# Linear attention and a multiplicative FFN on one core: a new slot plan for key features, query transposes and two numerators

## The chip, the cores and the metric

The kernel runs on one core of a Trainium2 chip. The metric is the device time in microseconds: the median of the runs of a kernel. The kernel before takes 248.61 us (three runs, 248.41 to 248.72).

## The reference

Eight batches of eight heads, 576 positions, head size 64. Queries and keys go through a ReLU and are multiplied by a cosine and by a sine of the position, which gives 128 features:

```python
    q_p = phi(q, cos_w, sin_w)
    k_p = phi(k, cos_w, sin_w)
    kv = np.einsum('bhsf,bhsd->bhfd', k_p, v)
    z = np.sum(k_p, axis=2)
    num = np.einsum('bhsf,bhfd->bhsd', q_p, kv)
    den = np.einsum('bhsf,bhf->bhs', q_p, z)[..., None] + 1e-06
```

The attention output `num / den` is laid out as 4608 tokens of 512 features and goes through an FFN without a nonlinearity: `h = (x @ w1) * (x @ w2)`, then `h @ w3 @ w_out`, where `w1` and `w2` are 512 x 1024, `w3` is 1024 x 1024 and `w_out` is 1024 x 512.

## The kernel before

Tokens pass the FFN in nine tiles of 512. `w3 @ w_out` is computed once, so a tile is: `x @ w1` and `x @ w2` (L465), a copy of the first product out of PSUM by ScalarE (L518), their product by VectorE into `abT` (L522), the output matmuls (L535), and a copy of the output by ScalarE (L542). The matmuls run in bf16.

Attention for a batch is cut into five chunks of positions (four of 128 rows, one of 64; odd batches take the chunk of 64 first). The steps for a chunk, and their names:

- key features, `prep_k`: cosine half on VectorE (L273), sine half on ScalarE (L277). They need the load of `ks`, which comes in two halves of the partitions; the chunk of 64 rows needs the first half alone.
- values copied by GpSimd, `prep_v` (L300).
- `kv_chunk` (L308): matmuls that sum keys times values over all five chunks in PSUM; the sum is copied to `kvs` (L313, L314).
- query features and their transpose, `prep_q`: features as for keys, then a transposing DMA from SyncE's queue into `qpT` (L286).
- numerators, `num` (L368): eight matmuls with `qpT` and `kvs`, then a normalization on VectorE in three instructions (L384 to L386) into `xblk`, which is read by `x_tr`, a transposing DMA (L416) on the same SyncE queue. This makes the `xT` that the FFN tiles read.

The order of the work is written out by hand. `ffn_groups` is a generator: after each group of matmuls of a tile (about four matmuls of 512 columns) it yields, and at that point the calls that are listed for this slot run, so attention instructions are put into each engine's queue between FFN instructions. There are 232 slots: 40 for tile 0, then 24 for each tile, 16 of L465 and 8 of L535. So slots 40 to 63 are tile 1, 64 to 87 tile 2, 88 to 111 tile 3, and so on. `plan` (L572) puts the five chunks of a batch at the slots given: `kf` for key features, `vc` for value copies, `kv` for the key-value sums, `qf` for query features with their transposes, `nu` for numerators. `plan_loads` (L584) places the loads of `k`, `q` and `v`, in halves. A load is held back by a tiny copy on ScalarE that GpSimd, whose queue issues the loads, waits for (L568, L570).

Batches 4 to 7 share one pattern: `last` is the slot of the first numerators of the batch before, `base` that of its own, and the places are offsets to one or the other. Every engine works its queue in the order that results, so an instruction that waits holds back all that stands behind it.

Of the kernel before, what the change touches and what calls it, by code (L numbers as in the profile page):

```python
# [68 lines left out]
def kernel(  # L69
# [176 lines left out]
    def order_of(b):  # L246

        return [0, 1, 2, 3, 4] if b % 2 == 0 else [4, 0, 1, 2, 3]
# [40 lines left out]
    def prep_k(b, c):  # L289
        features(b, feat_of(b)[0], raw[b, "k"], c)  # L290

    def prep_q(b, c):
        features(b, feat_of(b)[1], raw[b, "q"], c)
        if c in dma_q(b):
            transpose_q(b, c)

    def prep_v(b, c):
        R = ROWS[c]
        eng = nc.vector if b < 2 else nc.gpsimd
        eng.tensor_copy(out=feat_of(b)[2][:R, c, :, 0:D], in_=raw[b, "v"][:R, :, c, :])  # L300

    def kv_chunk(b, c, i):
        kp, qp, va = feat[b]
        if i == 0:
            att_of(b)["kv"] = ps_att.tile([P, 2, 512], FP32, name="pnum")
        kvt = att[b]["kv"]
        for h in range(H):
            nc.tensor.matmul(kvt[:, h // 4, ds((h % 4) * 65, 65)], lhsT=kp[:, c, h, :],  # L308
                             rhs=va[:, c, h, 0:D + 1], start=(i == 0 and h % 4 == 0),
                             stop=(i == NCH - 1 and h % 4 == 3))  # L310
        if i == NCH - 1:
            kvs = sm.tile([P, H, D + 1], BF16, name="kvs", bufs=2)
            nc.scalar.copy(out=kvs[:, 0:4, :], in_=kvt[:, 0, 0:260])  # L313
            nc.vector.tensor_copy(out=kvs[:, 4:8, :], in_=kvt[:, 1, 0:260])  # L314
            att[b]["kvs"] = kvs
# [88 lines left out]
    def x_tr(b, c, by_vector=False):  # L404
        R, rows = ROWS[c], out_rows(b, c)
        xblk = att[b]["x"].pop(c)
        xf = xblk[:].rearrange("p g h d -> p (g h d)")
        if b % 2 == 0:
            slot = S * b + 128 * c
        else:  # L410
            slot = S * b + (0 if c == 4 else 64 + 128 * c)
        t, o = divmod(slot, 512)
        if t not in xT:
            xT[t] = xtp.tile([P, 4, 512], BF16, name="xT")
        if b >= 2 or (b, c) in ((0, 4), (1, 3)):
            nc.sync.dma_start_transpose(out=xT[t][:, :, ds(o, R)], in_=xf[rows])  # L416
            return
        pst = ps_tr.tile([P, 8, 128], BF16, name="pst")
        for kc in range(4):
            nc.tensor.transpose(pst[:, kc, :], xf[:, ts(kc, 128)], identb[:])  # L420
        copy = nc.vector.tensor_copy if by_vector else nc.scalar.copy
        copy(out=xT[t][:, :, ds(o, R)], in_=pst[:, 0:4, rows])
# [139 lines left out]
    def at(s, *calls):  # L562
        slots[s] += calls
# [8 lines left out]
    def plan(b, kf, vc, kv, qf, nu, loads=None, xt=None):  # L572
        order = order_of(b)
        for i, c in enumerate(order):
            at(kf[i], lambda c=c: prep_k(b, c))
            at(qf[i], lambda c=c: prep_q(b, c))
            at(vc[i], lambda c=c: prep_v(b, c))
        for i, c in enumerate(order):
            at(kv[i], lambda c=c, i=i: kv_chunk(b, c, i))
        for i, c in enumerate(order):  # L580
            at(nu[i], lambda c=c: num(b, c, in_two=b == 1 and c in (0, 2)))
            at(xt[i] if xt else nu[i], lambda c=c: x_tr(b, c, by_vector=(b, c) == (1, 1)))

    def plan_loads(b, when):  # L584

        for piece, s in zip([(n, half) for n in {2: "kv", 3: "qkv"}.get(b, "kqv") for half in range(2)], when):
            def issue(piece=piece):
                hold_back()
                load(b, *piece)
            at(s, issue)  # L590
# [42 lines left out]
    for jp, s in enumerate((12, 16, 18, 20, 22, 24, 26, 28)):  # L633
# [3 lines left out]
         qf=(29, 30, 30, 31, 31), nu=(35, 36, 38, 39, 42), xt=(37, 38, 40, 42, 42))  # L637
    for c, s in zip(order_of(1), (31, 32, 34)):
# [3 lines left out]
    plan(2, kf=(37, 39, 40, 41, 44), vc=(41, 42, 43, 44, 45), kv=(46, 46, 46, 47, 47),  # L642
         qf=(41, 42, 43, 45, 46), nu=(48, 50, 52, 57, 60))
    plan_loads(3, (36, 37, 47, 50, 54, 57))
    plan(3, kf=(54, 57, 59, 61, 63), vc=(64, 65, 66, 67, 68), kv=(71, 71, 72, 72, 72),
         qf=(60, 62, 64, 67, 70), nu=(74, 77, 79, 84, 87))

    bases = [74, 99, 123, 148, 173]
    for b, last, base in zip(range(4, B), bases, bases[1:]):
        plan_loads(b, [last + s for s in (-11, -7, -4, 3, 6, 9)])  # L650
        plan(b, kf=[last + s for s in (3, 6, 8, 11, 13)],
             vc=[base + s for s in (-9, -8, -7, -6, -5)],
             kv=[base + s for s in (-4, -3, -3, -2, -2)],
             qf=[base + s for s in (-11, -9, -6, -4, -1)],
             nu=[base + s for s in (0, 2, 5, 8, 11)])

    for i in range(2 * (NT - 1)):
# [42 lines left out]
```

## Time and profile before

| what | value |
|---|---|
| time, median of three runs | 248.61 us |
| the profiled execution | 247.98 us, span 246.2 us |
| TensorE, share of the span | 97% |
| VectorE | 57% |
| ScalarE | 53% |
| GpSimd | 38% |
| HBM traffic over the span | 196 GB/s |

The share of the span is busy time; the ends of matmuls in the profile are modelled and overlap the next ones, so for TensorE it is read together with the starts of its instructions. The granted TensorE clock is full throughout. The chain of work that ended last is followed back from the end of the kernel; a line in it that is not TensorE's is a place where TensorE waited.

### The profile page before, as it was taken

The numbers are of one execution on the slowest core, as the hardware profiler recorded it, in microseconds if no ns is written. First come the engines' busy times: TensorE is split into PE (matmuls) and PEld (weight loads), VectorE is DVE, ScalarE is ACT, GpSimd is POOL, SyncE is SP. The second block draws the span as 40 slices with busy tenths as digits, with TensorE's granted clock in tenths as the row PEclk, the third lists the DMA queues.
The fourth block names the chain that finished last, engine by engine and source line by source line (L and its number), as shares of the span: only waits on it lengthen the run. The fifth ranks groups of instructions, "written<-read, shape, count | busy, mean of one in ns | idle before, by whom it ended". The sixth has DMA issues, their size and how long they took to land.

```text
span 246.2 us, 5011 instructions
## 1 busy us (share of the span) xinstructions
PE 238.2 (97%) x1842; PEld 130.7 (53%) x1872; DVE 139.3 (57%) x344; ACT 130.6 (53%) x266; POOL 94.2 (38%) x196
## 2 busy tenths in 40 slices
PE   8799999999999999999999999999999999999994
PEld 3479555566964445545554545455545544444443
DVE  7775663668975645655665575678466645312420
ACT  2675324856944873566367555754575333434332
POOL 7655352124412171218022804261303005978800
PEclk9999999999999999999999999999999999999999
DMA  7999999999989989999999999999996437988923
GB/s 192 179 197 199 207 206 201 192 185 167 167 146 143 164 117 164 155 124 136 177 161 133 142 140 162 158 132 169 151 120 122 63 64 219 256 284 282 284 109 128
DMA packets 86200, 41.22 MB, mean 167 GB/s; under 512 B 53792, under 2 KB 82720, under 8 KB 86176
## 3 DMA queue, kind: packets, MB, share of 16 engines
q0 software_dynamic: 37008, 27.20, 72.4%
q1 hardware_dynamic: 49168, 13.71, 38.0%
q8 instruction: 14, 0.23, 0.4%
q14 instruction: 10, 0.08, 0.1%
HBM read 38.80 MB, written 9.44 MB: 196 GB/s over the span
## 4 chain that ended last, share of the span: by engine, by line
PE 89%; DMA 5%; ACT 2%; DVE 1%; issue 1%; ACTq 0%
PE ffnps L465 48%; PE ffnps L535 24%; PE ffnps L240 6%; PE pnum L368 4%; PE pnum L308 4%; DMA ks<-in_k_dram 3%; DMA kf<-in_k_dram 3%; PE pst L226 1%; ACT kp L277 1%; PE pst L339 1%; PE pst L420 1%; PE ffnps L551 1%; PE kva L325 0%; DVE xblk L386 0%; DVE abT L522 0%
## 5 line engine op out<-in xcount | busy, mean ns | idle before, releaser
L465 PE MATMUL ffnps<-xT,w2b 128*128 128x512 bf16 (+2 forms) x337 | 75.0, 343 | 0.5
L465 PE MATMUL ffnps<-xT,w1b 128*128 128x512 bf16 (+2 forms) x335 | 74.5, 343 | 0.3
L522 DVE TENSOR_TENSOR abT<-asb,ffnps 128x512 bf16<-128x512 bf16 x64 | 43.9, 685 | 47.1 <-PE ffnps L465 44.8
L535 PE MATMUL ffnps<-w34b,abT 128*128 128x512 bf16 x270 | 63.6, 379 | 0.8 <-DVE abT L522 0.3
L518 ACT CAST asb<-ffnps 128x512 bf16<-128x512 f32 x64 | 37.4, 585 | 50.0 <-PE ffnps L465 42.8
L570 POOL COPY seen<-mark 1x1 bf16<-1x1 bf16 x50 | 9.2, 183 | 99.6 <-ACT mark L568 99.6
L465 PEld LDWEIGHTS <-w2b 128*128 128x128 bf16 x344 | 31.0, 98 | 27.3
L465 PEld LDWEIGHTS <-w1b 128*128 128x128 bf16 x344 | 30.9, 98 | 26.4
L535 PEld LDWEIGHTS <-abT 128*128 128x128 bf16 x280 | 25.9, 98 | 28.3 <-DVE abT L522 0.8
L542 ACT COPY osb<-ffnps 128x512 f32<-128x512 f32 x35 | 20.5, 585 | 34.8 <-PE ffnps L535 34.8
L277 ACT ACTIVATE qp<-qs,sinv 128x512 bf16<-128x512 bf16 (+2 forms) x40 | 28.1, 716 | 1.3 <-DMA qs<-in_q_dram 1.3
L386 DVE TENSOR_TENSOR xblk<-pnum,den 128x512 bf16<-128x512 f32 (+1 forms) x37 | 25.6, 691 | 1.3
L277 ACT ACTIVATE kp<-ks,sinv 128x512 bf16<-128x512 bf16 (+1 forms) x35 | 25.0, 720 | 1.6 <-DMA ks<-in_k_dram 1.6
L450 POOL DMA_DIRECT2D out_dram<-osb x42 | 22.1, 531 | 3.3 <-issue 2.5
L300 POOL COPY va<-vs 128x512 bf16<-128x512 bf16 (+1 forms) x30 | 17.4, 619 | 7.9 <-DMA vs<-in_v_dram 7.9
L368 PEld LDWEIGHTS <-qpT 128*128 128x128 bf16 x320 | 15.4, 98 | 8.6 <-DVE qpT L353 0.6
L384 DVE TENSOR_SCALAR den<-pnum 128x8 f32<-128x8 f32 (+1 forms) x37 | 6.1, 164 | 23.7 <-PE pnum L368 23.5
L273 DVE TENSOR_SCALAR qp<-qs,cosv 128x512 bf16<-128x512 bf16 (+1 forms) x40 | 18.6, 472 | 0.6 <-DMA qs<-in_q_dram 0.5
L368 PE MATMUL pnum<-kvs,qpT 128*128 128x65 bf16 x296 | 15.7, 194 | 0.1
L240 PE MATMUL ffnps<-woutb,w3T 128*128 128x512 bf16 x61 | 15.1, 379 | 0.2
L308 PEld LDWEIGHTS <-kp 128*128 128x128 bf16 x280 | 11.3, 98 | 3.8
L273 DVE TENSOR_SCALAR kp<-ks,cosv 128x512 bf16<-128x512 bf16 (+1 forms) x35 | 12.1, 358 | 1.7 <-DMA ks<-in_k_dram 1.6
(88 smaller groups left out, 182.6 us busy)
## 6 DMA issues: line engine op xcount, KB each, us to landing
out_dram<-osb POOLq DMA_DIRECT2D x16, 256.0 KB, 4.5
out_dram<-osb POOLq DMA_DIRECT2D x24, 128.0 KB, 4.0
qs<-in_q_dram POOLq DMA_DIRECT2D x8, 256.0 KB, 7.3
ks<-in_k_dram POOLq DMA_DIRECT2D x6, 320.0 KB, 7.0
qs<-in_q_dram POOLq DMA_DIRECT2D x6, 320.0 KB, 8.4
vs<-in_v_dram POOLq DMA_DIRECT2D x6, 320.0 KB, 6.0
ks<-in_k_dram POOLq DMA_DIRECT2D x6, 256.0 KB, 7.8
vs<-in_v_dram POOLq DMA_DIRECT2D x6, 256.0 KB, 5.9
```

Of the source, the lines that this page charges most:

```text
L240: nc.tensor.matmul(acc[:, :], lhsT=w3T[:, lc % 4, :], rhs=woutb[:, lc, :], start=(lc == 0), stop=(lc == 7))
L273: nc.vector.tensor_scalar(out=dst[:R, c, :, 0:D], in0=src[:R, :, c, :], scalar1=0.0, scalar2=cosv[:R, at:at + 1], op0=ALU.max, op1=ALU.mult)
L277: nc.scalar.activation(out=dst[:R, c, 0:n, D:F], in_=src[:R, 0:n, c, :], func=ACTF.Relu, scale=sinv[:R, at:at + 1], bias=0.0)
L308: nc.tensor.matmul(kvt[:, h // 4, ds((h % 4) * 65, 65)], lhsT=kp[:, c, h, :], rhs=va[:, c, h, 0:D + 1], start=(i == 0 and h % 4 == 0), sto ...
L368: nc.tensor.matmul(banks[h // 4][:, ds((h % 4) * 65, 65)], lhsT=qpT[:, h, ds(at, 128)], rhs=kvs[:, h, :], start=True, stop=True)
L386: nc.vector.tensor_tensor(out=xblk[rows, g], in0=n4[:, :, :, 0:D], in1=den[rows, g].unsqueeze(3).to_broadcast([R, G, 4, D]), op=ALU.mult)
L450: eng.dma_start(out=rows[:, :, cols], in_=osb[64 * i:64 * i + rows.shape[0], :, cols])
L465: nc.tensor.matmul(out, lhsT=w[:, kc, ts(jc, 128)], rhs=x[:, kc, tok], start=(kc == 0), stop=(kc == 3))
L518: nc.scalar.copy(out=asb[:], in_=aT[:, :])
L522: nc.vector.tensor_mul(out=abT[:, jc, :], in0=asb[:], in1=bT[:, :])
L535: nc.tensor.matmul(ops[:, :], lhsT=abT[:, jc, ts(ms, 128)], rhs=w34b[:, jc, :], start=(jc == 0), stop=(jc == 7))
L542: nc.scalar.copy(out=osb[:, ms % 2, :], in_=ops[:, :])
```

## The change

It gives other slots to attention work. In batch 3 the first key features move from slot 54 to 56, and the second and third numerators from 77 and 79 to 76 and 78. In batches 4 to 7 the key features after the first come one or two slots sooner, and the query features with their transposes one or two slots sooner, so that the last of them is at three slots ahead of the first numerators where it was one slot ahead. The aim is that data that pass through transposing transfers are there in time, and that a feature that waits for its load stands less in the way.

```diff
-    plan(3, kf=(54, 57, 59, 61, 63), vc=(64, 65, 66, 67, 68), kv=(71, 71, 72, 72, 72),
-         qf=(60, 62, 64, 67, 70), nu=(74, 77, 79, 84, 87))
+    plan(3, kf=(56, 57, 59, 61, 63), vc=(64, 65, 66, 67, 68), kv=(71, 71, 72, 72, 72),
+         qf=(60, 62, 64, 67, 70), nu=(74, 76, 78, 84, 87))
...
-        plan(b, kf=[last + s for s in (3, 6, 8, 11, 13)],
+        plan(b, kf=[last + s for s in (3, 5, 7, 9, 11)],
              vc=[base + s for s in (-9, -8, -7, -6, -5)],
              kv=[base + s for s in (-4, -3, -3, -2, -2)],
-             qf=[base + s for s in (-11, -9, -6, -4, -1)],
+             qf=[base + s for s in (-12, -10, -8, -6, -3)],
              nu=[base + s for s in (0, 2, 5, 8, 11)])
```

## The prediction

> **What bounds the kernel now.** I read the busy line of the page first, then the chain that ended last, then the list of waits, and last the timelines of TensorE and VectorE around the one wait in the middle. In order:
>
> ```profile
> PE 238.2 (97%) x1842; PEld 130.7 (53%) x1872; DVE 139.3 (57%) x344; ACT 130.6 (53%) x266; POOL 94.2 (38%) x196
> PE 89%; DMA 5%; ACT 2%; DVE 1%; issue 1%; ACTq 0%
> ```
>
> TensorE is busy 97% of the span and holds 89% of the chain that ended last. The modelled ends of matmuls overlap, so this busy share can hide small stalls; I measured them by starts. In steady stretches a 128x512 matmul starts 0.216 us after the one before it (four in 0.86 us). From 58 us to the last matmul at 243 us, every interval fits this rhythm (or twice it, at some twenty places where one record is missing) save two: 0.10 us at 70.3 us, ahead of batch 2's first numerator, and a larger one at 79 us. All else that a change in the middle of this kernel can win is that one, or lies in what this profile does not show. In the chain, the span of 246.2 us loses its time to transfers in two places:
>
> ```profile
> 0.74 6.18 DMA kf<-in_k_dram
> ...
> 70.72 7.33 DMA ks<-in_k_dram
> 78.11 0.28 issue
> 78.39 0.67 DVE abT L522
> 79.11 0.39 PE ffnps L535
> ```
>
> The first is the start-up, untouched here. The second is batch 3's key load, of which the chain says that it released VectorE, and VectorE released TensorE. The timelines, TensorE and then VectorE (start, duration, what; in brackets the idle time before it and who ended it):
>
> ```profile
> 76.24 1.03 PE L465 MATMUL ffnps<-xT,w2b 128*128 128x512 bf16 x4
> 77.11 1.67 PE L535 MATMUL ffnps<-w34b,abT 128*128 128x512 bf16 x7
> 79.11 0.39 PE L535 MATMUL ffnps<-w34b,abT 128*128 128x512 bf16 x1 [0.33 <-DVE abT L522]
> 79.33 0.42 PE L368 MATMUL pnum<-kvs,qpT 128*128 128x65 bf16 x8
> ```
>
> ```profile
> 75.76 0.68 DVE L522 TENSOR_TENSOR abT<-asb,ffnps 128x512 bf16<-128x512 bf16 x1
> 78.07 0.39 DVE L273 TENSOR_SCALAR kp<-ks,cosv 64x512 bf16<-64x512 bf16 x1 [1.63 <-DMA ks<-in_k_dram]
> 78.39 0.66 DVE L522 TENSOR_TENSOR abT<-asb,ffnps 128x512 bf16<-128x512 bf16 x1
> ```
>
> VectorE reached batch 3's first key feature (L273) at 76.44, and the load landed only at 78.05. Behind it stood the last product (L522) of FFN tile 1, though its inputs were there by about 77.3 (the w2 group starts at 76.24 and is over in about 1.03). The eighth output matmul needs that product. Seven matmuls from 77.11 put the eighth at 77.11 + 7 x 0.216 = 78.62; it started at 79.11. **The stall is 0.49 us** (0.33 as the profile counts it, since the modelled end of the seventh covers the rest). The waits list has nothing else of this kind, and for the query transposes that the change moves nothing but start-up work:
>
> ```profile
> DVE kp L273 <- DMA ks<-in_k_dram: 1.6, 1, 1.6
> PEld L535 <- DVE abT L522: 0.8, 1, 0.8
> PEld L368 <- DVE qpT L353: 0.6, 2, 0.4
> ```
>
> **What the Trainium skill says.** "TensorE: Matmul & The Clock Gate", section "Wait — 56ns, not 53.3ns?": start to start is N / 2.4 GHz + 2.5 ns, 215.7 ns at 512 columns. The trace agrees (0.216), so the matmul stream has no rate left to win. "Perfetto Trace Analysis", "Tensor Engine Instruction (MATMUL, LD_WEIGHTS)": matmul ends are estimated, and VectorE and ScalarE queues are strictly first in, first out. The trace agrees: the ready product waited behind the key feature. "DMA: Bandwidth & Descriptors", "Anatomy of one DMA — SWDGE (gpsimd) path": 2.0 us + bytes / 436e3, for 320 KB an estimate of 2.8 us. The trace disagrees: this load took 7.33, and the page's median for such loads is 7.0; I use the trace. Same page, "Issuing engines are not separate DMA queues": transposes and loads share 16 engines, which agrees with transposes taking 2.8 to 10.1 us between 131 and 176 us while loads run.
>
> **The change part by part.** No instruction is added or removed; the orders of GpSimd's and SyncE's queues stay as they were. Only places in the TensorE, VectorE and ScalarE orders move.
>
> Batch 3's first key chunk, slot 54 to 56. On VectorE the last product now stands ahead of the key feature. It can start at about 77.3 and end by 78.0, ahead of 78.62. TensorE gains 0.49 us. The wait is not gone: the feature still waits for 78.05, now with batch 2's fourth normalization (slot 57) behind it on VectorE. Its numerators run at 78.84 in the new clock (79.33 less 0.49), so VectorE is free first. On ScalarE the output copy of slot 57 stands behind the sine half, which ends at 78.8; its bank is reused only at slot 64, seven slots or some 6 us later. The second key chunk, slot 57 in both, waits for the second half (landed 80.87), now up to 0.49 us longer; behind it are output copies and batch 2's last normalization, none of which TensorE needs before slot 64. Cost nothing; **sum -0.49 us**.
>
> Batch 3's second and third numerators, slots 77 and 79 to 76 and 78. TensorE does the same eight matmuls each, 0.26 us, one 0.86 us group sooner. What is new: the third normalization (0.17 + 0.20 + 0.69, about 1.05 us) stands ahead of the last product of tile 2 on VectorE. On the old clock: numerators at 99.76, normalization free at 101.25, product 101.25 to 101.93; the output matmul that needs it issues at 100.89 + 7 x 0.216 = 102.40. Slack 0.4 us, so cost nothing (upper bound: if everything slips by 0.5, 0.1 us). What it buys: transposed x of batch 3's third chunk landed at 107.72, and tile 3 begins at 108.31, a slack of 0.6 us that grows by 0.8.
>
> Key features of batches 4 to 7, one or two slots sooner. Each is 0.36 on VectorE and 0.72 on ScalarE, beside output matmuls. Both halves of keys have landed before the first feature in each batch, by 3 us in batches 5 to 7; in batch 4 the second half lands at 98.62 and the first feature, whose slot does not change, runs on ScalarE at 98.65. That one is tight in both kernels. Cost nothing.
>
> Query features and transposes, one or two slots sooner. The second halves of q landed at 104.0, 129.0, 153.4 and 176.4; the first features ran at 109.8, 132.4, 157.0 and 181.0. One slot (about 0.9 us) fits. ScalarE then has a cast (0.58) and a feature (0.72) in each pair of slots of 1.73 us, VectorE 0.69 and 0.36; both fit. What it buys, by the completions in the trace: batch 5's fourth transpose landed at 150.29 for numerators at 150.90, batch 6's third and fourth at 171.66 and 174.75 for 172.19 and 175.04. Slacks of 0.6, 0.5 and 0.3 us grow by up to 1.7. In this profile that is worth zero. In the timed runs it may not be: their median, 248.61, is 0.63 above the profiled execution's 247.98, and late transfers are one thing that can fill this. Bounds 0 and 0.63; I take a fifth, 0.13, since fixed differences between the executions can fill it as well and three runs within 0.31 us do not look like chance stalls. This fifth is a judgment.
>
> Sum: -0.49 - 0.13 = -0.62, so 248.61 - 0.62 = **248.0 us**.
>
> **The rivals.**
> (A) The forecast, 248.0. For it: one stall, its cause named, its waiting product freed. Against: 0.49 is 0.197% of the time, at the very edge of what can be told, so all of the verdict hangs on the last tenths.
> (B) Only the stall, or part of it. The load's landing sets its size: if keys land 0.2 us earlier in timed runs, the stall there is 0.3. Then 248.61 - 0.3 to 0.49, about 248.2. For it: nothing else shows in the profile.
> (C) The near misses are real stalls in the timed runs. Then 0.49 + 0.63 = 1.12, 247.5. For it: three transposes within 0.6 us of their use; against: none stalls in the profile.
> (D) Slower. The transposes, packed two slots apart, take longer against the key loads issued at the same time, or the normalization ahead of tile 2's last product makes a new stall when batch 4's keys land late. A miss of about 1 us in one batch less the 0.49 gives +0.5, 249.1. For it: the tight landing at 98.62. Against: moves are all towards earlier, and the slacks above.
>
> **How the numbers follow.** A 0.50, B 0.27, C 0.13, D 0.10. Faster by over 0.2% (below 248.11): C and most of A, 0.42 + 0.13 = 0.55. Within: the rest of A, B, and 0.02 of D, 0.37. Slower: 0.08. The range leaves out half of C's and most of D's weight: 247.4 to 248.6.
>
> **What would show it.** The key-feature wait no longer stands ahead of the last product of tile 1, and the eighth output matmul follows at the 0.216 rhythm; the chain goes through no ks load in the middle; query transposes of batches 5 and 6 land 1 to 2 us ahead of their numerators; TensorE shows no new interval over 0.3 us. A new wait of an L535 or L368 matmul, or a span less than 0.3 us shorter, would prove me wrong.

## The result, and the profile after

The changed kernel takes 247.76 us (median of 15 runs, 247.51 to 248.43) against 248.72 us for the kernel before (15 runs, 247.67 to 249.65). The ratio is 0.9963, 95% interval 0.9949 to 0.9976: 0.9 us faster, and the spread of the runs is less than half as wide (0.9 us for 2.0). Two later comparisons of the same two kernels, below, gave a smaller gain, 0.6 to 0.7 us. Three later runs that took over 1.5% more than the fastest of their kernel, at a lowered clock, are left out of medians, means, counts and ratios: two of the kernel before and one of the larger dose.

The page of the changed kernel, its busy line and the line of the chain that ended last:

```profile
PE 238.0 (97%) x1842; PEld 130.7 (53%) x1872; DVE 138.2 (56%) x344; ACT 130.3 (53%) x266; POOL 94.1 (38%) x196
PE 92%; DMA 3%; issue 1%; DVE 1%; POOL 1%; ACT 0%; POOLq 0%
```

TensorE's share of the chain rises from 89% to 92%, and DMA's falls from 5% to 3%: a start-up load, now of queries and not of keys, is the only transfer left in it. The timelines of TensorE and VectorE around the old stall (start, duration, what; idle time before it in brackets):

```profile
76.39 1.03 PE L465 MATMUL ffnps<-xT,w2b 128*128 128x512 bf16 x4
77.25 1.89 PE L535 MATMUL ffnps<-w34b,abT 128*128 128x512 bf16 x8
78.98 0.42 PE L368 MATMUL pnum<-kvs,qpT 128*128 128x65 bf16 x8
```

```profile
75.91 0.68 DVE L522 TENSOR_TENSOR abT<-asb,ffnps 128x512 bf16<-128x512 bf16 x1
77.52 0.69 DVE L522 TENSOR_TENSOR abT<-asb,ffnps 128x512 bf16<-128x512 bf16 x1 [0.94 <-PE ffnps L465]
78.94 0.34 DVE L273 TENSOR_SCALAR kp<-ks,cosv 64x512 bf16<-64x512 bf16 x1 [0.72 <-DMA ks<-in_k_dram]
```

The eight output matmuls now stand in one row, x8 in 1.89 us, where they were x7 and, after a gap, x1. The product (L522) runs when TensorE has finished its inputs, at 77.52, and the key feature waits after it: 0.72 us on VectorE for 1.63 before. In total the two engines wait longer for key loads than before, where either waited 1.6 us, because in this execution the second half landed later too: VectorE waits 1.8 us and ScalarE 2.1 us for it.

```profile
ACT kp L277 <- DMA ks<-in_k_dram: 4.1, 3, 2.1
DVE kp L273 <- DMA ks<-in_k_dram: 2.5, 2, 1.8
```

The first half of batch 3's keys was issued at 70.86 and landed at 78.91, after 8.05 us for 7.33 in the profile of before. The second half landed at 82.29, after 8.42 us for 7.15. In the old order, by an estimate from the durations in the profile of before, the landing of the first half would have put the product at 79.27 to 79.93 and the eighth matmul at 79.98 for 78.76, a stall of 1.2 us. VectorE and ScalarE wait more for keys than they did, and TensorE does not wait for them at all: from 50 us on, its only interval out of rhythm is the 0.10 us at 70.4 that was there before.

The profiled spans differ by 0.34 us (246.22 and 245.88), not by 0.9: one execution each, and the changed one began its FFN 0.14 us later (first L465 at 16.01 for 15.87), so 0.34 + 0.14 is the 0.49 us stall to within 0.01.

### The profile page after: what moved, and what is told of

It is laid out like the page before. It is cut to its first block, busy times and chain, and to the rows that moved or that the text cites. A ratio compares the mean times of both kernels' runs of the same rounds, so it can differ in the third digit from the quotient of the medians.

```text
span 245.9 us, 5011 instructions
## 1 busy us (share of the span) xinstructions
PE 238.0 (97%) x1842; PEld 130.7 (53%) x1872; DVE 138.2 (56%) x344; ACT 130.3 (53%) x266; POOL 94.1 (38%) x196
## 4 chain that ended last, share of the span: by engine, by line
PE 92%; DMA 3%; issue 1%; DVE 1%; POOL 1%; ACT 0%; POOLq 0%
PE ffnps L465 50%; PE ffnps L535 24%; PE ffnps L240 6%; PE pnum L368 4%; PE pnum L308 4%; DMA qs<-in_q_dram 3%; PE pst L226 1%; PE pst L339 1%; PE pst L420 1%; PE ffnps L551 1%; POOL vs L133 0%; DVE xblk L386 0%; PE pfirst L368 0%; PE ffnps L368 0%; DVE qpT L353 0%
## 5 line engine op out<-in xcount | busy, mean ns | idle before, releaser
L465 PE MATMUL ffnps<-xT,w2b 128*128 128x512 bf16 (+2 forms) x337 | 75.0, 343 | 0.5
L465 PE MATMUL ffnps<-xT,w1b 128*128 128x512 bf16 (+2 forms) x335 | 74.5, 343 | 0.3
L522 DVE TENSOR_TENSOR abT<-asb,ffnps 128x512 bf16<-128x512 bf16 x64 | 43.9, 685 | 49.1 <-PE ffnps L465 44.8
L465 PEld LDWEIGHTS <-w2b 128*128 128x128 bf16 x344 | 30.9, 98 | 26.8
L465 PEld LDWEIGHTS <-w1b 128*128 128x128 bf16 x344 | 30.9, 98 | 26.6
L273 DVE TENSOR_SCALAR qp<-qs,cosv 128x512 bf16<-128x512 bf16 (+1 forms) x40 | 16.7, 425 | 0.7 <-DMA qs<-in_q_dram 0.7
```

The source lines that it names most:

```text
L273: nc.vector.tensor_scalar(out=dst[:R, c, :, 0:D], in0=src[:R, :, c, :], scalar1=0.0, scalar2=cosv[:R, at:at + 1], op0=ALU.max, op1=ALU.mult)
L465: nc.tensor.matmul(out, lhsT=w[:, kc, ts(jc, 128)], rhs=x[:, kc, tok], start=(kc == 0), stop=(kc == 3))
L522: nc.vector.tensor_mul(out=abT[:, jc, :], in0=asb[:], in1=bT[:, :])
```

## The experiments

Two theories. **Theory 1**: all of the gain is the key-load stall, whose size varies with the landing. **Theory 2**: the stall is part of it, and the rest is transposing transfers that in some executions land after TensorE needs them. The kernels were measured in three groups, each on one chip together with the kernel before; each entry gives the ratio to the kernel before of its group. A profile is one execution, and several of those below are among the longest of their kernel, so a wait in them shows what can happen and not what is usual.

**The first key feature alone.**

```diff
-    plan(3, kf=(54, 57, 59, 61, 63), ...
+    plan(3, kf=(56, 57, 59, 61, 63), ...
```

> Kernel before, with batch 3's first key feature at slot 56 instead of 54 and nothing else. Theory 1 (the whole gain is the key-load stall at the end of FFN tile 1, which is 0.5 us in the profile and larger in most timed runs): about 0.9 us faster than before, ratio 0.9963, and no interval over 0.3 us between matmul starts in the middle. Theory 2 (the stall gives its profiled 0.49 us, the rest comes from query transposes that miss their numerators in timed runs): 0.4 to 0.5 us faster, ratio about 0.998.

Measured: 247.86 us, ratio 0.9966 (0.9947 to 0.9985). That is nearest to what theory 1 expected, though the interval holds theory 2's 0.998 as well; either way most of the gain is here. But its profile was taken in a long execution, 249.28 us, and shows a wait that the other moves of the change are meant against:

```profile
108.62 0.42 PE L368 MATMUL pnum<-kvs,qpT 128*128 128x65 bf16 x8
109.52 1.04 PE L465 MATMUL ffnps<-xT,w1b 128*128 128x512 bf16 x4 [0.48 <-DMA xT<-xblk]
```

Tile 3 starts at 109.52 where the rhythm has 108.88: 0.64 us lost to `xT`. The chain of that stretch goes back to the transfer, issued behind the normalization of batch 3's third chunk and landed at 109.48:

```profile
102.50 0.69 DVE xblk L386
103.20 0.03 DVE kp L273
103.22 6.25 DMA xT<-xblk
109.48 0.05 issue
109.52 2.55 PE ffnps L465 x11
```

It is the transfer that had 0.6 us of slack in the profile of before. In the same profile tile 2 began 0.53 us late: its last piece of x landed at 85.35, some 0.3 us after the tile was due, and the tile started at 85.60. The profile puts the end of this wait down to ScalarE; that the late x was the cause is read from the landing. So slacks of a few tenths are losses in some executions.

**All but the first key feature.** The changed kernel with `kf=(54, ...` for batch 3.

> Changed kernel with batch 3's first key feature back at slot 54; numerators, later keys and query transposes stay moved. Theory 1: the same as before, ratio 1.000, with the stall of about 0.5 to 1 us back at the eighth output matmul of tile 1. Theory 2: 0.4 us faster than before, ratio 0.998, the stall being there as well.

Measured: 248.50 us, ratio 0.9986 (0.9966 to 1.0006), which leaves both theories standing. Most of the gain is gone, and the profile has the stall back:

```profile
77.30 1.67 PE L535 MATMUL ffnps<-w34b,abT 128*128 128x512 bf16 x7
79.30 0.39 PE L535 MATMUL ffnps<-w34b,abT 128*128 128x512 bf16 x1 [0.33 <-DVE abT L522]
```

x7 and x1 again, 0.49 us.

**The same wait taken away by an earlier load.**

```diff
-    plan_loads(3, (36, 37, 47, 50, 54, 57))
+    plan_loads(3, (36, 37, 45, 47, 54, 57))
```

> Kernel before with batch 3's key loads issued two and three slots sooner (slots 45 and 47 for 47 and 50); the features stay at 54. Takes the wait away by another means. Theory 1: the first half lands about 2 us sooner, so the feature waits little or not at all; the stall goes and the gain is the same as with the later feature, 0.9 us, ratio 0.9963. If the landing only moves with the traffic (it crowds with query transposes and lands as late as before), no gain, ratio 1.000. Theory 2: 0.4 to 0.5 us.

Measured: 250.07 us, ratio 1.0055 (1.0032 to 1.0078): 1.3 us slower, which neither theory expected. The key did land early (first half at 74.46), and the key stall is gone: the eight output matmuls are in one row. TensorE loses more elsewhere (the profile is that of the longest of its 19 runs, 252.02 us):

```profile
75.26 0.43 PE L368 MATMUL pnum<-kvs,qpT 128*128 128x65 bf16 x8 [0.97 <-DMA qpT<-qp]
...
78.12 1.89 PE L535 MATMUL ffnps<-w34b,abT 128*128 128x512 bf16 x8
80.75 0.43 PE L368 MATMUL pnum<-kvs,qpT 128*128 128x65 bf16 x8 [0.74 <-DMA qpT<-qp]
```

Two numerators of batch 2 wait for their query transposes, by starts 1.14 and 0.90 us. (Two of batch 4 wait as well, 0.24 and 1.24 us, in a part that this edit does not touch.) The chain of the stretch:

```profile
70.09 10.61 DMA qpT<-qp
80.70 0.05 issue
80.75 0.43 PE pnum L368 x8
```

A transpose issued at 70.09 took 10.61 us and landed at 80.70; the second half of the keys, issued at 70.44, landed at 80.66. The load that was moved forward now runs beside batch 2's third and fourth transposes. They took 6.49 and 10.61 us here, and 3.3 to 4.1 and 5.0 to 8.5 us in the twelve profiles with the load in its old place. The wait went from a load to a transpose, and got longer. That shows the mechanism of theory 2 at work, in a kernel that brings it about; it does not size it in the kernel before.

**A larger dose.** The kernel before with `kf=(52, 57, ...` for batch 3.

> Kernel before with batch 3's first key feature two slots sooner still, 52. A dose: now two products and one cast of tile 1 stand behind the waiting feature. If the landing stays at 78.05 us: products at 78.4 and, behind a cast that ends at 79.3, at 79.3 to 80.0, so the eighth output matmul starts at about 80.05 for 78.62: a stall of 1.4 us in place of 0.5, 0.9 us slower than before, ratio 1.004. Both theories expect it; if it costs nothing, the stall is no part of the bound and both fall.

Measured: 249.41 us, ratio 1.0029 (1.0005 to 1.0054), 0.7 us slower for 0.9 expected. VectorE and then TensorE in its profile, which is that of its longest run (252.48 us):

```profile
78.60 0.34 DVE L273 TENSOR_SCALAR kp<-ks,cosv 64x512 bf16<-64x512 bf16 x1 [3.02 <-DMA ks<-in_k_dram]
78.87 0.67 DVE L522 TENSOR_TENSOR abT<-asb,ffnps 128x512 bf16<-128x512 bf16 x1
79.82 0.69 DVE L522 TENSOR_TENSOR abT<-asb,ffnps 128x512 bf16<-128x512 bf16 x1 [0.28 <-ACT asb L518]
```

```profile
76.84 1.46 PE L535 MATMUL ffnps<-w34b,abT 128*128 128x512 bf16 x6
79.60 0.39 PE L535 MATMUL ffnps<-w34b,abT 128*128 128x512 bf16 x1 [1.29 <-DVE abT L522]
80.57 0.39 PE L535 MATMUL ffnps<-w34b,abT 128*128 128x512 bf16 x1 [0.58 <-DVE abT L522]
...
179.52 0.43 PE L368 MATMUL pnum<-kvs,qpT 128*128 128x65 bf16 x8 [1.21 <-DMA qpT<-qp]
```

Two products stand behind the feature, and TensorE waits twice, 1.46 and 0.75 us by starts. The load landed at 78.58 here, 8.12 us after its issue. The first key feature's place does set the time. The last line is another matter: batch 6's fourth transpose, one of the three that the prediction named as near misses, took 12.14 us in this execution, and its numerators lost 1.37 us by starts.

**The full change and the first key feature alone, on one chip.** Both as they were.

> The changed kernel itself, unaltered, to stand on one chip beside the first key feature's move alone. Theory 1 (the key-load stall is the whole of it): the same median as that move alone, within 0.1 us, and as wide a spread. Theory 2 (the other moves give slack to transfers whose landing varies from execution to execution; in the profile of the move alone, tile 3 waited 0.64 us for the transposed x of batch 3's third chunk): median 0.1 to 0.3 us below the move alone, and few or no runs over 248.5, where the move alone had 8 of 22.

> Batch 3's first key feature at slot 56 and nothing else, as before, on the same chip as the full change. Theory 1: as the full change. Theory 2: a median 0.1 to 0.3 us above it and a third of the runs over 248.5.

Measured: 247.75 us, ratio 0.9977 (0.9963 to 0.9991), one of 22 runs over 248.5; and 247.85 us, ratio 0.9979 (0.9961 to 0.9996), seven of 22 over 248.5, as many as in the first group (seven there as well, not the eight that the expectation names). The medians differ by 0.1 us and the means by 0.17, 95% interval -0.08 to 0.43, so these alone do not tell the two kernels apart; the count of long runs, one for seven, speaks for theory 2. The profile of the first key feature's move alone shows one of those, in a batch whose transposes the change moves:

```profile
123.75 1.03 PE L535 MATMUL ffnps<-w34b,abT 128*128 128x512 bf16 x4
125.41 0.43 PE L368 MATMUL pnum<-kvs,qpT 128*128 128x65 bf16 x8 [0.63 <-DMA qpT<-qp]
```

Batch 4's third transpose, issued at 115.83, landed at 125.36; its numerators lost 0.79 us, and the second ones 0.27 just before.

**The two numerators of batch 3.** The first key feature's move, and `nu=(74, 76, 78, 84, 87)`.

> The first key feature's move and batch 3's two numerators one slot sooner, later batches as before. Theory 2: the wait of tile 3's first matmuls for batch 3's third x is gone from any profile; the waits for query transposes of batches 5 and 6 stay possible, so the spread lies between the move alone and the full change. Theory 1: all three alike.

Measured: 247.92 us, 14 runs, three over 248.5, ratio 0.9992 (0.9975 to 1.0009). No wait of tile 3 in its profile, but the times don't tell it from the first key feature alone.

**The opposite of the change for the transposes.**

```diff
-             qf=[base + s for s in (-11, -9, -6, -4, -1)],
+             qf=[base + s for s in (-9, -7, -4, -2, 1)],
```

> The first key feature's move, and in batches 4 to 7 the query features with their transposes two slots later than before (the last at one slot behind the first numerators), the opposite of the change. In the profile of before the transposes of batch 5's fourth and batch 6's third and fourth chunk landed 0.6, 0.5 and 0.3 us ahead of their numerators. Two slots are 1.7 us and more, so if the landings move along, three numerators wait 1.1 to 1.4 us each, partly absorbed by one another: 1.5 to 3 us slower than the first key feature's move alone, with waits for qpT ahead of numerators of batches 5 and 6. Theory 1 as stated (transposes have slack to spare): no slower than the move alone.

(The first key feature was at 56 here.) Measured: 248.85 us, ratio 1.0014 (0.9995 to 1.0034): 1.0 us over the first key feature's move alone on the same chip, less than the 1.5 to 3 expected, and 14 of 22 runs over 248.5. By means it is 0.83 us, 95% interval 0.46 to 1.24. In its profile, again a long execution (250.42 us), one numerator of batches 4 to 7 waits where three were expected, and tile 3 waits as well:

```profile
108.88 1.04 PE L465 MATMUL ffnps<-xT,w1b 128*128 128x512 bf16 x4 [0.64 <-DMA xT<-xblk]
...
147.82 1.03 PE L535 MATMUL ffnps<-w34b,abT 128*128 128x512 bf16 x4
150.22 0.43 PE L368 MATMUL pnum<-kvs,qpT 128*128 128x65 bf16 x8 [1.37 <-DMA qpT<-qp]
```

Batch 5's third numerators lose 1.53 us by starts, and tile 3, which still has batch 3's numerators in their old places, 0.80 us. Slack that is taken from the transposes is paid for, about 1 us in the median. That contradicts theory 1 as the expectation states it, that the transposes have slack to spare; what added slack gains it does not measure.

**The change without the numerators of batch 3, and more of the same.** The first is the changed kernel with `nu=(74, 77, 79, 84, 87)`; the second is this edit:

```diff
-         qf=(41, 42, 43, 45, 46), nu=(48, 50, 52, 57, 60))
+         qf=(41, 42, 43, 45, 46), nu=(48, 50, 51, 58, 61))
...
-             qf=[base + s for s in (-12, -10, -8, -6, -3)],
+             qf=[base + s for s in (-13, -11, -9, -7, -4)],
```

> The changed kernel with batch 3's two numerators back at slots 77 and 79, so the first key feature's move and the earlier keys, queries and transposes of batches 4 to 7 remain. If the query transposes carry what the first key feature's move leaves over: as the full change, median 247.75 and one or two of 22 runs over 248.5. If batch 3's numerators carry it: as the first key feature's move alone, about a third of the runs over 248.5. With both at work it lies between.

> The changed kernel with more of the same: query features and transposes of batches 4 to 7 one slot sooner again; batch 2's third numerators one slot sooner (its x landed 0.95 us ahead of tile 2 in the changed kernel) and its last two one slot later (a transpose landed 0.27 us ahead of the fourth numerators). If late transfers are all that is left above the lowest time, the slowest runs come down: no run over 248.4, median 247.6 to 247.7, lowest unchanged at 247.4 to 247.5. If the rest lies elsewhere (start-up), as the changed kernel.

> The changed kernel, unaltered, on the same chip as the two others, for comparison: median 247.7 to 247.9, one run in twenty over 248.5, lowest 247.4 to 247.5.

Measured: 247.77 us with none of 22 runs over 248.5, ratio 0.9984 (0.9971 to 0.9997); 247.88 us with three of 14 over 248.5, ratio 0.9987 (0.9963 to 1.0011); and for the change itself 247.66 us with two of 22, ratio 0.9967 (0.9952 to 0.9982). More of the same is no better than the change.

All runs together, where the kernel before itself had medians of 248.25 to 248.72 by group, so that tenths between different groups are not firm:

| kernel | runs | lowest | median | mean | over 248.5 |
|---|---|---|---|---|---|
| before | 195 | 247.33 | 248.50 | 248.61 | 96 |
| first key feature alone | 44 | 247.42 | 247.86 | 248.08 | 14 |
| that and batch 3's numerators | 14 | 247.54 | 247.92 | 248.06 | 3 |
| that and batches 4 to 7 | 22 | 247.36 | 247.77 | 247.80 | 0 |
| the full change | 59 | 247.41 | 247.74 | 247.81 | 3 |

The lowest times agree within 0.21 us in all rows, which can be read as the time with no transfer late. By this reading, which no run tests, the change does not shorten the work; it brings more executions to it.

Against the kernel before of the same group, the first key feature gave 0.70 and 0.50 us by means (0.86 and 0.56 by medians), and the full change 0.93 us in the section on the result and then 0.68 and 0.64 (0.96, 0.66 and 0.59). All but the first key feature gave 0.23 us by means, with an interval that holds zero (-0.14 to 0.58). So the rest of the change is worth some 0.1 to 0.3 us, and its size is not firm.

The profiles, though few, point the same way. Of the six with the query transposes of batches 4 to 7 in their old places, three have numerators of these batches that lose 0.2 us or more to a late transpose (the first key feature alone in the second group, the earlier load and the larger dose); of the six with the places of the change or sooner, none. The last piece of x for tile 3 was late in two of the seven with batch 3's numerators in their old places and in none of the six with the new. Together with the count of long runs this speaks against theory 1 in its strict form; theory 2 stands, with the size of its second part open. Of the rest, the runs point to batches 4 to 7 (0 of 22 long runs for 14 of 44, though on different chips). Whether batch 3's numerators shorten the median stays open.

## Why the prediction was right

It said 248.0 us, 247.4 to 248.6, faster; measured 247.76. The gain was put at 0.62 us and came out as 0.96 by medians in this comparison, from a kernel before that took 0.11 us more than the three runs that the forecast started from; the two later comparisons gave 0.66 and 0.59. The range was wide enough to hold nearly no gain as well.

- The stall and its cause, first term: shown. The move of one feature gives it, putting the feature back brings the stall back, and a larger dose makes it larger. Its size, 0.49 us, was read from one execution, and over the runs the move gives 0.50 to 0.70 by means. The load landed 6.1 to 8.1 us after its issue in the profiles, and by the estimate above a landing after 8.05 us is a stall of 1.2 us, so one profile's stall is a draw, not the size; that this draw lay so near the mean was luck.
- The slacks of a few tenths in the transposes and in batch 3's x, second term: right in kind. They are waits in some executions and none in others. The 0.13 lies within the 0.1 to 0.3 that the runs allow, but the reason for so little does not hold: three runs within 0.31 us were read as speaking against chance stalls, and 15 runs of the same kernel spread over 2.0 us. So rival C is true in part: late transposes exist, but most executions don't have them, and 0.63 us was too much. Which transpose is nearly late changes from execution to execution. The three that the prediction named landed 0.3 to 0.6 us ahead in the profile of before, and 1.3 to 2.8 us ahead in three other profiles with the old places (the first key feature alone, both times, and with batch 3's numerators), while in one of these it was batch 4's that came late. In the changed profile they land 2.6 us (batch 5's fourth), 2.6 and 3.5 us (batch 6's third and fourth) ahead of their numerators, and batch 3's third x 2.4 us ahead of tile 3.
- The terms at nothing: held. The normalization ahead of tile 2's last product, the tight landing of batch 4's keys and the copies behind batch 3's second key half cost TensorE no interval in the changed profile, though ScalarE waited 2.1 us for that half (landed 82.29).
- Rival B, the stall alone: the first key feature's kernel is this case, 247.86 and 247.85. It was put at 248.2, too high for the same reason as in the first point.
- Rival D, slower: its mechanism, transposes crowded by key loads, is real, but it came with the earlier load of an experiment, not with the change.

## What to carry to other kernels

An instruction that waits for a transfer should stand behind the last instruction of its engine that the bounding engine needs soon; here moving it two slots back cost nothing and gave most of the gain. Look for what lands within a few tenths of its use, not just for waits: one execution shows some of the late transfers, the spread of the runs shows the rest. Starting a load sooner is not the same as needing it later: here it then ran beside transfers that were due sooner, and they came late.

## What was not expected of the hardware

A transpose that is issued ahead of a load can land with it: 70.09 to 80.70 beside a load of 70.44 to 80.66. The Trainium skill, "DMA: Bandwidth & Descriptors", section "Issuing engines are not separate DMA queues", says that both run on the same 16 engines and interleave, and this agrees.

In the larger dose's profile, the stretch of TensorE's two waits and the one after it (length; busy time of TensorE, its weight loads, VectorE, ScalarE and GpSimd; then the granted clock, the DMA share, in which packets that overlap all count, and GB/s):

```profile
78.00:81.00 3.00, 1.13 (x9) 0.42 (x8) 1.63 (x3) 1.29 (x4) 0.71 (x2) 0.98 1.58 163
81.00:85.00 4.00, 4.00 (x18) 1.68 (x16) 1.80 (x5) 1.76 (x4) 0.99 (x3) 0.59 1.18 128
```

TensorE worked 1.13 of 3 us, and then had a granted clock of 0.59 for 4 us, with matmuls 0.427 us apart for 0.216. Summed over starts, the slower matmuls lost 1.7 us, beside the 2.2 us of the two waits; that the waits brought the clock down is inferred from their order. A single wait was followed by no such drop: after the 1.37 us at 179.5 in the same profile, and after the 1.53 us in that of the later transposes, the granted clock stayed at 1.00. The Trainium skill, "TensorE: Matmul & The Clock Gate", section "HAM oscillation — how this bites in real kernels", gives a fall of the clock for idle gaps beyond some 3.4 us; here neither gap was over 1.5 us, and the measurement decides. It was seen in one profile, of that kernel's longest run, and its cause stays open.
